# Four sums of squares split by one instruction per engine and multiplied with w_out one period later

## The chip, the cores and the metric

The kernel runs on one core of a Trainium2 chip. The metric is the device time of one execution in microseconds, the median of three runs. The engines go by the profile's names: PE is TensorE (PEld its weight loads), DVE is VectorE, ACT is ScalarE, POOL is GpSimd, and SP is the engine whose queue issues most of the transfers.

## The reference

Channel attention followed by a feed-forward layer with a squared ReLU, for 4 batches of 6080 tokens and 256 channels:

```
qn = q / (norm(q over tokens) + 1e-6);  kn likewise
a  = softmax(kn^T @ qn / tau)                 # 256 x 256 for each batch
x  = v @ a, read as 24320 rows of 256
h  = max(x @ w_in, 0)                         # 2048 columns
out = (h * h) @ w_out                         # back to 256
```

All values are float32. `w_in` and `w_out` arrive as 64-bit words that the kernel decodes.

## The kernel before, in words

The attention matrix of a batch is multiplied into `w_in`, so that each batch has its own weights W = a @ w_in, and the feed-forward layer reads v directly. Every float32 operand is split into a rounded part ("hi") and the rest ("lo"), both of the type float32r, and a product is three matmuls: hi with hi, hi with lo, lo with hi.

The tokens of a batch are cut into 12 blocks of 512 (the last two of 480). The first two blocks and the very last one are done plainly. The 45 blocks between run in 180 periods, four for each block (`groups`, with k the period and j = 0 to 3 the quarter of the 2048 hidden columns). A period forms its quarter by a Strassen-like scheme (Winograd's variant): seven products of 6 matmuls, accumulated in three PSUM banks, B2 (`h0`), H (`h1`) and C (`h2`). In the program's order these are B2 = A11 B11 and H = S1 T1; then, with C first set to a copy of B2 by ACT, C += S2 T2, B2 += A12 B21, H += S4 B22, C += S3 T3 and, last, C += A22 T4. Between them ACT and DVE take the four results a1, a0, a2, a3 out of PSUM into the tile `x` (with ReLU), and square them. The second product, with w_out, works on four sums of these squares (`first_sums`, `third_sum`, `last_sum`, on DVE) and on some of the squares themselves (the "A" parts).

The order of the work on each engine is the order in which the program issues it (`InProgramOrder`, L19 to L27: nearly every instruction has L27 as its line, so that the tiles' names tell the operations apart). The period (L1250) interleaves three periods' work:

- of period k: the seven products, the evictions, ReLU and squares, and the early A parts (`hi_A(k, early_A)`, `lo_A`);
- of period k-1: the sums, the split of the late A part, the split of the four sums in two steps (`hi_S` on ACT and `lo_S` on DVE for "S1", which is a1 and a0, and again for "S2", which is a2 and a3), `window_A(k - 1)` on PE before the last product of C, and `window_S(k - 1, "S1")` on PE at the end of the period;
- of period k-2: `window_S(k - 2, "S2")` on PE between the product H = S1 T1 and C += S2 T2.

A quarter is "plain" (`plain(k)`) when its odd pair of column groups is multiplied without the scheme: j = 0 and 1 in the first three batches, and all of the first such block. A plain quarter has 9 matmuls in `window_A` and 18 and 15 in the two halves of `window_S`; another one has 18, 12 and 12.

`after_copy(k)` (L1246) decides where ACT rounds the late A part: where it holds (the last batch, not plain), after the copy of B2 into C of the next period; elsewhere ahead of it, at the end of the period itself (L1332). In the first case DVE runs `first_sums` ahead of `lo_A`, in the other behind it.

The weights of a period come by transfers on SP's queue in two loads (`load_forms`): the early ones (A11, S1, S2) are issued two periods ahead, the late ones one period ahead; each is two transfers, hi and lo. The attention of the next batch runs beside the periods in steps that wait for named points (`side("act")`, `"mid"`, `"dve"`, `"sq"`, `"pe"`): 12 matmuls of its Gram matrix in a period, and after that the norms and the softmax. The norms (`ps_n`, L600) use B2's bank `h0`: PE forms them at the point "act", ahead of `window_A`, and DVE reads them (`nx`, L616) at the point "mid", behind the split of the sums.

After the last period the plain last block starts (L1501): its steps run beside the windows that are left over (`drained`).

Of the kernel before, what the change touches and what calls it, by code (L numbers as in the profile page):

```python
# [30 lines left out]
def kernel(  # L31
# [843 lines left out]

    def two_parts(name, tag, src):

        hi, lo = [pool.tile(list(src.shape), F32R, tag=f"{tag}_{i}", name=f"{tag}_{i}{name}", bufs=1) for i in ("hi", "lo")]

        def round_hi():  # L880
            scalar.copy(hi, src)

        def take_lo():
            vector.tensor_sub(lo, src, hi.bitcast(F32))

        return hi, lo, round_hi, take_lo

    def parts_of(b, n, r):

        hi, lo, round_hi, take_lo = two_parts(f"{b}_{n}_{r}", ("s1", "s2")[r % 2], X.pop((b, n, r)))  # L890
        round_hi()
        take_lo()
        G[b, n, r] = hi, lo
# [3 lines left out]
    def eight_products(b, n, r, part):  # L897
        t0, tn = blocks[n]
        f = 2 * r + part
        if f == 0:  # L900
            O[b, n] = ps_acc.tile([P, NC, T], F32, tag="o", name=f"ps_o{b}_{n}")
        hi, lo = (x.rearrange("p s t -> p (s t)")[:, part * tn : (part + 1) * tn] for x in G[b, n, r])
        parts = ((wo_hi, hi), (wo_lo, hi), (wo_hi, lo))
# [22 lines left out]
    def final_products(b, n, r, part):  # L926
# [6 lines left out]
        hi, lo = (x.rearrange("p s t -> p (s t)") for x in G[b, n, r])  # L933
        ends = r == NPAIR - 1
# [22 lines left out]
    OLD = 2  # L957
    ORD = 1
    AT = (0, 0, 24, 26)
    AFTER_FROM = (12, 12, 12, 0)  # L960
    FREE_FROM = (12, 12, 12, 0)
# [43 lines left out]
    def half_of(k):  # L1005
        return blocks[groups[k][1]][1] // 2
# [75 lines left out]

    def window_S(k, which):
        j = groups[k][2]
        names = {"S1": ((1, "S1n"), (2, "S3")), "S2": ((0, "S2"), (3, "A22"))}[which]
        pairs = range(1 if plain(k) else 2)
        sums = [
            (1, at, 1, weights_of(2 * j + p)[name], p, slot) for slot, (at, name) in enumerate(names) for p in pairs
        ]
        if plain(k):  # L1090
            r = 2 * j + 1
            f = int(which == "S2")
            w = [[w[:, 2 * r + f, m * P : (m + 1) * P] for w in (wo_hi, wo_lo)] for m in range(2)]
            if f == 0:
                sums += [(0, 3, 1, w[0], 1, 0), (0, 2, 1, w[0], 1, 1)]
            else:
                sums.append((0, 2, 2, w[0], 1, 0))
            for slot, side in enumerate(((1, 0), (0, 1))[f]):
                t, at = ((0, 0), (1, 3))[side]
                sums.append((t, at, 1, w[1], 1, slot))  # L1100
        to_output(k, sums, PA[k, which])

# [82 lines left out]

    SLOTS = {"S1": slice(a1, a0 + 1), "S2": slice(a2, a3 + 1)}

    def parts_tile(k, kind):
        n = 3 if kind == "A" else 2
        tag = {"A": "A", "S1": "s1", "S2": "s2"}[kind]  # L1190
        PA[k, kind] = [
            pool.tile([P, 2, n, half_of(k)], F32R, tag=f"{tag}_{i}", name=f"{tag}_{i}_{k}", bufs=1) for i in ("hi", "lo")
        ]
# [6 lines left out]
    def lo_A(k, which):  # L1200
        s, at = which
        n = 1 if plain(k) else 2
        hi, lo = (part[:, 0:n, at, :] for part in PA[k, "A"])
        vector.tensor_sub(lo, XG[k][:, 0:n, s, :], hi.bitcast(F32))

    def hi_S(k, which):
        parts_tile(k, which)
        scalar.copy(PA[k, which][0], XG[k][:, :, SLOTS[which], :])

    def lo_S(k, which):  # L1210
        hi, lo = PA[k, which]
        vector.tensor_sub(lo, XG[k][:, :, SLOTS[which], :], hi.bitcast(F32))

# [31 lines left out]

    def after_copy(k):  # L1246

        return not plain(k) and k < len(groups) - 1 and groups[k][1] >= AFTER_FROM[groups[k][0]]

    def period(k, before=nothing, w1=None, wa=None, w3=None):  # L1250

# [18 lines left out]
        if prev:  # L1270
            if ORD and after_copy(k - 1):
                first_sums(k - 1)
                lo_A(k - 1, late_A)
            else:
# [48 lines left out]
        parts_tile(k, "A")  # L1323
        hi_A(k, early_A)
# [126 lines left out]
    for g in range(len(groups)):  # L1451
        b, n, j = groups[g]
        if g == 0:
            period(
                g,
                before=lambda: parts_of(*pairs[-1]),
                w1=left_over((PAIR // 2 - 2, 0), (PAIR // 2 - 2, 1)),
                wa=left_over((PAIR // 2 - 1, 0)),
                w3=left_over((PAIR // 2 - 1, 1)),
            )  # L1460
        elif g == 1:
            period(g, w1=nothing)
        else:
            period(g)
# [5 lines left out]
    banks["turn"] = 0  # L1470
    def sums_of_last():
        first_sums(K - 1)
        lo_A(K - 1, late_A)
        third_sum(K - 1)
        last_sum(K - 1)
        hi_S(K - 1, "S1")
        lo_S(K - 1, "S1")

    def rest_of_last():
        hi_S(K - 1, "S2")  # L1480
        lo_S(K - 1, "S2")

    drained = {
        0: (
            lambda: window_S(K - 2, "S2"),
            sums_of_last,
# [3 lines left out]
        ),  # L1490
        1: (lambda: window_A(K - 1), rest_of_last),
        2: (lambda: window_S(K - 1, "S1"),),
        3: (
            lambda: window_S(K - 1, "S2"),
            lambda: copy_output(K - 1, 0),
# [51 lines left out]
```

## Time and profile before

| | us |
|---|---|
| median of 3 runs (2137.43 to 2138.04) | 2137.51 |
| span of the profiled execution | 2137.0 |
| PE busy (16990 matmuls) | 2123.9 |
| PE weight loads busy (16990) | 2066.1 |
| DVE busy (2577 instructions) | 1947.1 |
| ACT busy (2708 instructions) | 1818.6 |
| POOL busy | 403.4 |

The page names the execution by its span. Busy time is the union of an engine's instructions, so matmuls that overlap in the pipeline count once. In the timeline a line gives the start, the length, the engine, the operation and its tiles; the bracket at the end is the idle time of the engine just before, with what ended it. The granted TensorE clock is 1.000 over the span. The chain that ended last is PE for 89%, DVE for 6%, ACT and the transfers for 2% each.

### The profile page before, as it was taken

What the parts mean: (1) busy time and instruction counts of PE and PEld (TensorE: products, weight loads), DVE (VectorE), ACT (ScalarE), POOL (GpSimd) and SP (SyncE); (2) the same over time, 40 slices, a digit from 0 to 9 for tenths busy, and PEclk for the clock granted to TensorE, in tenths of its full rate; (3) what the DMA queues carried; (4) which work ended last, traced back from release to release, by engine and by line L of the source; (5) the groups of instructions that cost most, each with busy time, mean ns of one, the idle gap of its engine ahead of it and who ended that gap; (6) DMA issues with size and microseconds to landing.
All of it is one profiled execution on the core that took longest, in us unless ns stands there. A gap on an engine that the chain in (4) does not pass through costs nothing.

```text
span 2137.0 us, 43905 instructions
## 1 busy us (share of the span) xinstructions
PE 2123.9 (99%) x16990; PEld 2066.1 (97%) x16990; DVE 1947.1 (91%) x2577; ACT 1818.6 (85%) x2708; POOL 403.4 (19%) x506
## 2 busy tenths in 40 slices
PE   9999999999999999999999999999999999999999
PEld 8789999999999999999999999999999999999998
DVE  6898999998999999988999999999899999999993
ACT  5887888888888888878888888878888999999995
POOL 0000121211222121221222121121212122122121
PEclk9999999999999999999999999999999999999999
DMA  9777888889998888788999788887999788788783
GB/s 345 234 232 264 240 255 252 235 239 283 303 297 262 251 251 262 234 241 247 292 303 288 248 255 257 249 234 229 325 322 314 233 241 252 220 247 248 233 256 86
DMA packets 258865, 548.24 MB, mean 257 GB/s; under 512 B 26848, under 2 KB 120672, under 8 KB 258656
## 3 DMA queue, kind: packets, MB, share of 16 engines
q1 hardware_dynamic: 193696, 449.32, 62.3%
q0 software_dynamic: 64960, 96.11, 20.9%
q8 instruction: 134, 2.20, 0.4%
q14 instruction: 75, 0.61, 0.1%
HBM read 431.75 MB, written 64.23 MB: 232 GB/s over the span
## 4 chain that ended last, share of the span: by engine, by line
PE 89%; DVE 6%; ACT 2%; DMA 2%; issue 1%; SPq 0%; DVEq 0%; ACTq 0%
PE ps_o L27 41%; PE ps_c L27 16%; PE ps_h L27 14%; PE ps_b L27 11%; PE gram L27 4%; DVE x L27 2%; PE ps_w L27 2%; PE ps_o_m L27 1%; ACT x L27 1%; DMA wf<-wf_kept 1%; DVE s_lo L27 1%; DVE acc L27 1%; DMA qk<-in_k 1%; DVE A_lo L27 0%; DMA qk<-in_q 0%
## 5 line engine op out<-in xcount | busy, mean ns | idle before, releaser
L27 DVE TENSOR_TENSOR s_lo<-x,s_hi 128x1024 fp32r<-128x1024 f32 (+1 forms) x384 | 464.0, 1208 | 44.4 <-ACT s_hi L27 44.1
L27 PE MATMUL ps_c<-v_hi,wf 128*128 128x256 f32 (+1 forms) x2160 | 466.9, 280 | 4.4 <-DVE x L27 2.2
L27 POOL DMA_DIRECT2D o<-o x225 | 245.4, 1253 | 1102.7 <-ACT o L27 689.7
L27 ACT CAST s_hi<-x 128x1024 fp32r<-128x1024 f32 (+1 forms) x384 | 399.7, 1041 | 37.6 <-DVE x L27 27.9
L27 DVE TENSOR_TENSOR x<-x 128x1024 f32<-128x1024 f32 (+3 forms) x540 | 389.6, 722 | 10.3
L27 PEld LDWEIGHTS ps_c<-v_hi,wf 128*128 128x128 f32 x2160 | 367.4, 188 | 7.8 <-ACT ps_c L27 3.3
L27 ACT ACTIVATE x<-x 128x512 f32<-128x512 f32 (+2 forms) x540 | 350.0, 648 | 21.7 <-DVE x L27 9.2
L27 PE MATMUL ps_b<-v_hi,wf 128*128 128x256 f32 (+1 forms) x1440 | 309.7, 279 | 1.8 <-DVE nx L27 1.1
L27 PE MATMUL ps_h<-v_hi,wf 128*128 128x256 f32 (+1 forms) x1440 | 309.1, 278 | 0.0
L27 PE MATMUL ps_c<-v_lo,wf 128*128 128x256 f32 (+1 forms) x1080 | 300.9, 279 | 0.0
L27 DVE TENSOR_TENSOR A_lo<-x,A_hi 128x1024 fp32r<-128x1024 f32 (+3 forms) x360 | 276.9, 792 | 18.8 <-ACT A_hi L27 15.3
L27 ACT CAST A_hi<-x 128x1024 fp32r<-128x1024 f32 (+3 forms) x360 | 254.4, 707 | 38.4 <-DVE x L27 25.5
L27 PEld LDWEIGHTS ps_b<-v_hi,wf 128*128 128x128 f32 x1440 | 245.2, 188 | 2.3 <-DVE nx L27 1.3
L27 PEld LDWEIGHTS ps_h<-v_hi,wf 128*128 128x128 f32 x1440 | 244.9, 188 | 0.0
L27 ACT COPY x<-ps_c 128x512 f32<-128x512 f32 (+1 forms) x180 | 105.1, 584 | 158.3 <-PE ps_c L27 158.0
L27 PEld LDWEIGHTS ps_c<-v_lo,wf 128*128 128x128 f32 x1080 | 203.2, 188 | 0.1
L27 PE MATMUL ps_b<-v_lo,wf 128*128 128x256 f32 (+1 forms) x720 | 200.6, 279 | 0.0
L27 PE MATMUL ps_h<-v_lo,wf 128*128 128x256 f32 (+1 forms) x720 | 200.4, 278 | 0.0
L27 DVE TENSOR_TENSOR x<-x,ps_h 128x512 f32<-128x512 f32 (+1 forms) x180 | 122.4, 680 | 76.9 <-PE ps_h L27 76.6
L27 PE MATMUL ps_o<-s_hi,wo_hi 128*128 128x256 f32 (+3 forms) x954 | 190.1, 295 | 0.5 <-ACT s_hi L27 0.5
L27 PE MATMUL ps_o<-s_hi,wo_lo 128*128 128x256 f32 (+3 forms) x954 | 190.2, 295 | 0.0
L27 PE MATMUL ps_o<-s_lo,wo_hi 128*128 128x256 f32 (+3 forms) x954 | 190.0, 295 | 0.1
(166 smaller groups left out, 5166.9 us busy)
## 6 DMA issues: line engine op xcount, KB each, us to landing
wf<-wf_kept SPq DMA_DIRECT2D x360, 512.0 KB, 5.3
wf<-wf_kept SPq DMA_DIRECT2D x360, 384.0 KB, 4.9
o<-o POOLq DMA_DIRECT2D x114, 256.0 KB, 5.9
qk<-in_k SPq DMA_DIRECT2D x87, 256.0 KB, 4.3
qk<-in_q SPq DMA_DIRECT2D x87, 256.0 KB, 4.8
v<-in_vT POOLq DMA_DIRECT2D x76, 256.0 KB, 5.1
out_T<-o POOLq DMA_DIRECT2D x152, 128.0 KB, 4.7
o<-o POOLq DMA_DIRECT2D x76, 128.0 KB, 6.2
```

What stands on the lines that cost most here:

```text
L27: return lambda *args, **kwargs: self.tc.keep_in_program_order(issue(*args, **kwargs))
```

## The change

The split of the four sums becomes one instruction on ACT (`scalar.copy` of 128x2048) and one on DVE (`tensor_sub` of 128x2048), from and into one pair of tiles `s_parts` in place of the four tiles of "S1" and "S2". Both come later in the period: `hi_S(k - 1)` behind the eviction of a0 and the copy of the second half of an output, `lo_S(k - 1)` behind `relu_squares`. For that `last_sum` is always done with `third_sum`, ahead of the addition of H to a1. `window_S` is one window, placed where the "S2" half stood: in period k it multiplies the sums of k-2. The window at the period's end is gone. `after_copy` is gone: the late A part is rounded behind the copy of B2 into C, and `first_sums` runs ahead of `lo_A`, in all periods. The plain blocks at the beginning and the end use halves of `s_parts`; the last block has a third pair of buffers, in the place of A's tiles. The drained windows at the end move with it.

```
-    def window_S(k, which):
+    def window_S(k):
...
         sums = [
-            (1, at, 1, weights_of(2 * j + p)[name], p, slot) for slot, (at, name) in enumerate(names) for p in pairs
+            (1, at, 1, weights_of(2 * j + p)[name], p, slot)
+            for at, name, slot in ((1, "S1n", a1), (2, "S3", a0), (0, "S2", a2), (3, "A22", a3))
+            for p in pairs
         ]
...
-    def hi_S(k, which):
-        parts_tile(k, which)
-        scalar.copy(PA[k, which][0], XG[k][:, :, SLOTS[which], :])
-
-    def lo_S(k, which):
-        hi, lo = PA[k, which]
-        vector.tensor_sub(lo, XG[k][:, :, SLOTS[which], :], hi.bitcast(F32))
+    def hi_S(k):
+        half = half_of(k)
+        PA[k, "S"] = [part[:, : 8 * half].rearrange("p (r s t) -> p r s t", r=2, s=4) for part in s_parts]
+        scalar.copy(PA[k, "S"][0], XG[k])
+
+    def lo_S(k):
+        hi, lo = PA[k, "S"]
+        vector.tensor_sub(lo, XG[k], hi.bitcast(F32))
...
         scalar.copy(C[:, :, :half], B2[:, :, :half])
-        if prev and after_copy(k - 1):
+        if prev:
             hi_A(k - 1, late_A)
...
         if prev:
-            if ORD and after_copy(k - 1):
-                first_sums(k - 1)
-                lo_A(k - 1, late_A)
-            else:
-                lo_A(k - 1, late_A)
-                first_sums(k - 1)
+            first_sums(k - 1)
+            lo_A(k - 1, late_A)
         side("dve")
         late_step(last=True)
         if prev:
             third_sum(k - 1)
-            if plain(k - 1):
-                last_sum(k - 1)
+            last_sum(k - 1)
         v_step(k, "dve")
-        (w1 or (lambda: window_S(k - 2, "S2")))()
+        (w1 or (lambda: window_S(k - 2)))()
...
         product(k, B2, A12, B21)
-        if prev:
-            hi_S(k - 1, "S1")
         scalar.activation(x[:, :, a0, :], B2[:, :, :half], AF.Relu)
         if w1 is None:
             copy_output(k - 2, 1)
+        if prev:
+            hi_S(k - 1)
         product(k, H, S4, B22)
...
-        if prev and not plain(k - 1):
-            last_sum(k - 1)
         product(k, C, S3, T3)
...
         side("sq")
-        if prev:
-            lo_S(k - 1, "S1")
-            hi_S(k - 1, "S2")
         square(k, a0)
         relu_squares(k)
         if prev:
-            lo_S(k - 1, "S2")
+            lo_S(k - 1)
...
         square(k, a2)
-        if not after_copy(k):
-            hi_A(k, late_A)
-        (w3 or (lambda: window_S(k - 1, "S1")))()
```

## Rows read from the trace of the kernel before

**Rows 1.** The page's head and its part 1: busy time, share of the span and instructions of each engine.
```profile
span 2137.0 us, 43905 instructions
...
PE 2123.9 (99%) x16990; PEld 2066.1 (97%) x16990; DVE 1947.1 (91%) x2577; ACT 1818.6 (85%) x2708; POOL 403.4 (19%) x506
```

**Rows 2.** Busy time in a stretch, here the periods: the stretch, its length, busy us and instructions of each engine, granted clock, transfer share, GB/s.
```profile
160.00:2076.00 1916.00, 1909.32 (x15982) 1887.76 (x15981) 1790.92 (x2381) 1663.09 (x2511) 383.86 (x476) 1.00 0.85 260
```

**Rows 3.** Waits of PE's weight loads in the periods (160 to 2076 us): who waited, for whom, us in total, times, the longest.
```profile
PEld ps_c L27 <- ACT ps_c L27: 3.3, 6, 1.1
PEld ps_c L27 <- DVE x L27: 3.2, 5, 1.1
PEld ps_b L27 <- DVE nx L27: 1.3, 1, 1.3
PEld ps_b L27 <- DMA wf<-wf_kept: 0.9, 1, 0.9
```

**Rows 4.** Timeline, DVE and PE, about 416 to 418.5 us (the norms of the second batch, between two periods). The first two lines are DVE, the others PE.
```profile
416.43 1.22 DVE L27 TENSOR_TENSOR s_lo<-x,s_hi 128x1024 fp32r<-128x1024 f32 x1
417.56 0.15 DVE L27 TENSOR_SCALAR nx<-ps_n 128x4 f32<-128x4 f32 x1
...
416.36 0.39 PE L27 MATMUL ps_o<-s_hi,wS_hi 128*128 128x256 f32 x2
...
418.45 0.28 PE L27 MATMUL ps_b<-v_hi,wf 128*128 128x256 f32 x1
```

**Rows 5.** The same for the third batch's norms, 919 to 927 us.
```profile
919.71 0.69 DVE L27 TENSOR_TENSOR x<-x,ps_h 128x512 f32<-128x512 f32 x1 [1.09 <-PE ps_h L27]
920.32 0.68 DVE L27 TENSOR_TENSOR x<-x 128x512 f32<-128x512 f32 x1
...
926.64 0.15 DVE L27 TENSOR_SCALAR nx<-ps_n 128x4 f32<-128x4 f32 x1
...
924.17 0.28 PE L27 MATMUL ps_o<-s_hi,wS_hi 128*128 128x256 f32 x1
...
926.85 0.38 PE L27 MATMUL ps_b<-v_hi,wf 128*128 128x256 f32 x1 [1.11 <-DVE nx L27]
```

**Rows 6.** The same for the fourth batch's norms, 1429 to 1431.5 us.
```profile
1430.48 0.15 DVE L27 TENSOR_SCALAR nx<-ps_n 128x4 f32<-128x4 f32 x1
...
1429.28 0.40 PE L27 MATMUL ps_o<-s_hi,wS_hi 128*128 128x256 f32 x2
...
1431.40 0.28 PE L27 MATMUL ps_b<-v_hi,wf 128*128 128x256 f32 x1
```

**Rows 7.** Timeline, PE, 1134 to 1137 us (end of a period and begin of the next).
```profile
1134.50 0.27 PE L27 MATMUL ps_o<-s_hi,wS_hi 128*128 128x240 f32 x1
...
1135.84 0.28 PE L27 MATMUL ps_b<-v_hi,wf 128*128 128x256 f32 x1
...
1136.96 0.50 PE L27 MATMUL ps_b<-v_hi,wf 128*128 128x256 f32 x2 [0.73 <-DMA wf<-wf_kept]
```

**Rows 8.** Timeline, PE, 628 to 630.5 us; then the transfers issued from 622.6 to 622.8 us and from 624.4 to 624.6 us (the early weights, hi and lo, of the period that begins at 630.27: issuer, count, size, us from issue to landing).
```profile
628.15 0.40 PE L27 MATMUL ps_o<-s_hi,wS_hi 128*128 128x256 f32 x2
...
630.27 0.28 PE L27 MATMUL ps_b<-v_hi,wf 128*128 128x256 f32 x1
...
wf<-wf_kept SPq DMA_DIRECT2D x1, 384.0 KB, 5.7
...
wf<-wf_kept SPq DMA_DIRECT2D x1, 384.0 KB, 5.5
```

**Rows 9.** Groups of instructions by form over the span: DVE's and ACT's splits, x the count, then busy us, mean ns of one, idle before.
```profile
L27 DVE TENSOR_TENSOR s_lo<-x,s_hi 128x1024 fp32r<-128x1024 f32 x320 | 390.3, 1220 | 15.1 <-ACT s_hi L27 15.0
...
L27 ACT CAST s_hi<-x 128x1024 fp32r<-128x1024 f32 x320 | 335.9, 1050 | 20.9 <-DVE x L27 20.8
...
L27 DVE TENSOR_TENSOR A_lo<-x,A_hi 128x512 fp32r<-128x512 f32 x152 | 104.3, 686 | 11.9 <-ACT A_hi L27 11.7
...
L27 ACT CAST A_hi<-x 128x512 fp32r<-128x512 f32 x152 | 94.6, 622 | 18.5 <-DVE x L27 11.3 <-PE ps_c L27 5.5
```

**Rows 10.** Timeline, ACT, 725 to 737 us: a period with j = 3 in the stretch in which the Gram matrix runs beside, up to the copy of B2 into C of the next period.
```profile
726.31 1.05 ACT L27 CAST s_hi<-x 128x1024 fp32r<-128x1024 f32 x1
...
727.97 1.30 ACT L27 ACTIVATE x<-x 128x512 f32<-128x512 f32 x2
729.17 1.05 ACT L27 ACTIVATE qk<-qk 128x1024 f32<-128x1024 f32 x1
730.12 1.03 ACT L27 CAST s_hi<-x 128x1024 fp32r<-128x1024 f32 x1
...
734.77 0.62 ACT L27 CAST A_hi<-x 128x512 fp32r<-128x512 f32 x1
735.29 0.58 ACT L27 COPY ps_c<-ps_b 128x512 f32<-128x512 f32 x1
```

**Rows 11.** The same stretch on DVE (third sum, addition of H to a1, last sum), and the matmul on PE that waits for the copy.
```profile
726.33 0.68 DVE L27 TENSOR_TENSOR x<-x 128x512 f32<-128x512 f32 x1
727.24 0.69 DVE L27 TENSOR_TENSOR x<-x,ps_h 128x512 f32<-128x512 f32 x1 [0.23 <-PE ps_h L27]
727.85 0.68 DVE L27 TENSOR_TENSOR x<-x 128x512 f32<-128x512 f32 x1
...
736.09 0.28 PE L27 MATMUL ps_c<-v_hi,wf 128*128 128x256 f32 x1
```

More of the change, by code (lines that the diff above doesn't have):

```diff
@@ L874, in squares @@
         scalar.activation(x, x, AF.Square)
[L876 to L886, printed above, removed]
-    def parts_of(b, n, r):
-        hi, lo, round_hi, take_lo = two_parts(f"{b}_{n}_{r}", ("s1", "s2")[r % 2], X.pop((b, n, r)))
-        round_hi()
-        take_lo()
+    s_parts = [pool.tile([P, 4 * T], F32R, tag=f"s_{i}", name=f"s_{i}", bufs=1) for i in ("hi", "lo")]
+    def parts_of(b, n, r):
+        src = X.pop((b, n, r)).rearrange("p s t -> p (s t)")
+        tn = blocks[n][1]
+        at = r % 3 if (b, n) == order[-1] else r % 2
+        if at == 2 and "A" not in G:
+            G["A"] = [pool.tile([P, 2 * tn], F32R, tag=f"A_{i}", name=f"A_{i}_last", bufs=1) for i in ("hi", "lo")]
+        hi, lo = G["A"] if at == 2 else (part[:, 2 * tn * at : 2 * tn * (at + 1)] for part in s_parts)
+        scalar.copy(hi, src)
+        vector.tensor_sub(lo, src, hi.bitcast(F32))
         G[b, n, r] = hi, lo
@@ L901, in eight_products @@
             O[b, n] = ps_acc.tile([P, NC, T], F32, tag="o", name=f"ps_o{b}_{n}")
-        hi, lo = (x.rearrange("p s t -> p (s t)")[:, part * tn : (part + 1) * tn] for x in G[b, n, r])
+        hi, lo = (x[:, part * tn : (part + 1) * tn] for x in G[b, n, r])
         parts = ((wo_hi, hi), (wo_lo, hi), (wo_hi, lo))
@@ L932, in final_products @@
                 final[m] = ps_acc.tile([P, T], F32, tag="o", name=f"ps_o{b}_{n}_m{m}")
-        hi, lo = (x.rearrange("p s t -> p (s t)") for x in G[b, n, r])
+        hi, lo = G[b, n, r]
         ends = r == NPAIR - 1
@@ L957 @@
     OLD = 2
-    ORD = 1
     AT = (0, 0, 24, 26)
-    AFTER_FROM = (12, 12, 12, 0)
     FREE_FROM = (12, 12, 12, 0)
@@ L1091, in window_S @@
             r = 2 * j + 1
[L1092 to L1095, printed above, removed]
-            else:
[L1097 to L1101, printed above, removed]
+            w = [[[w[:, 2 * r + f, m * P : (m + 1) * P] for w in (wo_hi, wo_lo)] for m in range(2)] for f in range(2)]
+            sums += [(0, 3, 1, w[0][0], 1, a1), (0, 2, 1, w[0][0], 1, a0), (0, 2, 2, w[1][0], 1, a2)]
+            sums += [(1, 3, 1, w[0][1], 1, a1), (0, 0, 1, w[0][1], 1, a0)]
+            sums += [(0, 0, 1, w[1][1], 1, a2), (1, 3, 1, w[1][1], 1, a3)]
+        to_output(k, sums, PA[k, "S"])
     def copy_output(k, t):
@@ L1184, in last_sum, with parts_of_A @@
         sum_of(k, a3, a3, a2, vector.tensor_sub)
[L1186 to L1192, printed above, removed]
+    def parts_of_A(k):
+        PA[k, "A"] = [
+            pool.tile([P, 2, 3, half_of(k)], F32R, tag=f"A_{i}", name=f"A_{i}_{k}", bufs=1) for i in ("hi", "lo")
         ]
@@ L1244, in v_step, with period @@
         next(vprep[0], None)
-    def after_copy(k):
-        return not plain(k) and k < len(groups) - 1 and groups[k][1] >= AFTER_FROM[groups[k][0]]
-    def period(k, before=nothing, w1=None, wa=None, w3=None):
+    def period(k, before=nothing, w1=None, wa=None):
         now["k"] = k
@@ L1270, in period @@
         if prev:
-            if ORD and after_copy(k - 1):
-                first_sums(k - 1)
-                lo_A(k - 1, late_A)
-            else:
-                lo_A(k - 1, late_A)
-                first_sums(k - 1)
+            first_sums(k - 1)
+            lo_A(k - 1, late_A)
         side("dve")
@@ L1322, in period @@
         (wa or (lambda: window_A(k - 1)))()
-        parts_tile(k, "A")
+        parts_of_A(k)
         hi_A(k, early_A)
@@ L1458 @@
                 wa=left_over((PAIR // 2 - 1, 0)),
-                w3=left_over((PAIR // 2 - 1, 1)),
             )
         elif g == 1:
-            period(g, w1=nothing)
+            period(g, w1=left_over((PAIR // 2 - 1, 1)))
         else:
@@ L1471, in sums_of_last @@
     def sums_of_last():
+        hi_A(K - 1, late_A)
         first_sums(K - 1)
@@ L1475, in sums_of_last @@
         last_sum(K - 1)
[L1476 to L1481, printed above, removed]
+        hi_S(K - 1)
+        lo_S(K - 1)
     drained = {
         0: (
-            lambda: window_S(K - 2, "S2"),
+            lambda: window_S(K - 2),
             sums_of_last,
@@ L1490 @@
         ),
-        1: (lambda: window_A(K - 1), rest_of_last),
-        2: (lambda: window_S(K - 1, "S1"),),
+        1: (lambda: window_A(K - 1),),
         3: (
-            lambda: window_S(K - 1, "S2"),
+            lambda: window_S(K - 1),
             lambda: copy_output(K - 1, 0),
```

1 line of the change is left out of this document (removed).

## The prediction

> **What bounds the kernel now.** I read the page's busy times first, then the busy time of the periods alone, then what PE waited for in them, and only then single periods in the timeline. The page shows PE busy for 2123.9 of 2137.0 us, DVE for 91% and ACT for 85% [rows 1]. From 160 to 2076 us PE is busy for 1909.3 of 1916.0 us, so that 6.7 us are idle there, while DVE has 125 us and ACT 253 us to spare [rows 2]. PE's matmuls start one behind the other at 0.116 us for 256 columns: 18 of them from 416.36 to 418.45 us [rows 4]. So PE sets the end. The change leaves the count and the form of its matmuls as they are; it can move the time only by PE's waits. Those in the periods are few: its weight loads waited 3.3 us in 6 places for ACT's copy of B2 into C, 3.2 us in 5 places for DVE, 1.3 us once for DVE's reading of the norms and 0.9 us once for a transfer of weights [rows 3]. A gain can come from the first two only. The reader is to look for the places where a wait that is now hidden loses its cover.
>
> **What moves on PE.** From C += A22 T4 of a period to B2 = A11 B11 of the next PE now has the "S1" window to do: 18 matmuls (2.09 us) behind a plain quarter [rows 4], 12 behind another (1.40 us at 0.1165). After the change B2 stands directly behind the last product of C, and these matmuls come 12 matmuls later. All anchors from C += S2 T2 on keep their distance, since A and both halves of S still lie between one H += S4 B22 and the next. So the deadlines of B2 = A11 B11 alone are 1.4 to 2.1 us earlier, and whatever is ready less than that ahead of it now is late. B2's bank is free by then in an ordinary period (its eviction lies before `window_A`). Two kinds of producer are not.
>
> **The norms.** In three periods, one for each of the batches 2 to 4, the bank holds `ps_n` until DVE has read it, at a point behind the split of the sums.
> - 417 us: DVE reads at 417.56, PE is through with A22 at 416.36 and has the S1 window until 418.45 as cover [rows 4]. Without it B2 starts when the reading has ended. DVE's order up to there is the same work, 0.07 us shorter (below): 417.56 - 0.07 + 0.15 and 0.06 for the release, which is what lies between the end of the reading at 926.79 and the matmul at 926.85 [rows 5], is 417.70. PE waits for 1.34 us.
> - 1430 us: the same, 1430.48 - 0.07 + 0.15 + 0.06 = 1430.62 against 1429.28 [rows 6]: 1.34 us.
> - 926 us: B2 waits already, until 926.85 [rows 5]. The S1 window of 1.40 us that is done before this now comes after it. Against that DVE comes there earlier: `last_sum` (0.61 us from the start of the one before) now stands between the additions of H and C to the results; moved ahead it falls into 1.09 us in which DVE waits for PE [rows 5]. I take 0.50 of it, as the addition of C can't start before its product is done, and 0.07 from the split: 1.40 - 0.57 = 0.83 us.
> Together 3.5 us; at least 2.5 (if DVE gains 0.4 us in each), at most 4.1 (no gain at all).
>
> **The weights.** The early weights are wanted by B2 = A11 B11, and their transfers are issued by SP behind other work, not by PE's new order.
> - 1136 us: the third matmul of B2 waits for the lo half until 1136.96; the S1 window lay from 1134.50 to 1135.84 [rows 7]. The landing stays where it is, so the 1.34 us come on top.
> - 628 us: B2 starts at 630.27 and would start at 628.15; the hi half, issued at about 622.7, lands 5.7 us later, at 628.4, and the lo half, issued at about 624.45, 5.5 us later, at 629.95 [rows 8]. The third matmul, 0.23 us behind the first, then starts at 630.0 in place of 628.38: 1.6 us.
> Together 3.0 us; none if SP's queue comes to these loads 2 us earlier (it waits there for DVE steps that gain some 0.1 to 0.3 us, so hardly), 4 if the load at 1136 is late by one more us.
>
> **The split by one instruction.** No instruction of 128x2048 is in the trace. On DVE 128x512 takes 686 ns and 128x1024 takes 1220, on ACT 622 and 1050 [rows 9]; continued on the same line, 2048 takes 2288 and 1906 ns. What counts is the distance of starts: 1.13 us on DVE for 1024 [rows 4], 0.95 on ACT [rows 10], 0.09 and 0.10 less than the duration. So two now cost 2.27 and 1.90 us, one then 2.20 and 1.80: 0.07 and 0.10 us saved in a period, 12 and 18 us over 180. The bounds are no saving (two starts) and the whole fixed part, 1220 - 2 x 534 = 152 ns and 1050 - 2 x 428 = 194 ns. All of it lies beside PE. [...]
>
> **The order on ACT and DVE.** The late A part's rounding goes behind the copy of B2 into C: 0.52 us earlier for the copy [rows 10]. But the first half of the split now runs while ACT would stand idle: at 726.31, ahead of the relu that waits for DVE's addition at 727.97 [rows 10]. The one instruction has to wait for `last_sum`. DVE's row has third sum, addition, last sum at 726.33, 727.24 and 727.85 [rows 11]; moved ahead, the last sum ends at about 727.5. The split then runs from 727.6 to 729.4, and the relu follows 1.4 us later than before. What was behind it loses the second split (0.95 us) and the rounding (0.52 us and the wait for the square that feeds it, some 0.1). Net: the copy starts 0 to 0.2 us earlier than at 735.29. It is done at 735.87 and wanted at 736.09 [rows 10, 11], so 0.2 us of slack hold in this kind of period, of which a batch has about six beside its Gram matrix, 18 in three batches. Where DVE is later, as in the places of the six waits, I expect the copy between 0.5 us earlier and 0.3 us later, 0.7 us won over the six; from DVE's waits 0.15 us in each of five, 0.7 us; and 0.6 us from DVE's other short delays of PE. Together 2.0 us won; the bounds are all of the 6.5 us [rows 3], and 2 us lost.
>
> `lo_A` and `first_sums` change places at no cost: the same DVE work, and what waits for it (third sum, `window_A`) is behind both. The S window's operands are ready a whole half period before it starts, so the later splits cost PE nothing; the cover is PE's own B2 and H. The copies of the outputs and the third buffer pair of the last block stand on ACT and DVE where PE has work. POOL's and SP's queues are passed by nothing new.
>
> **The sum.** 3.5 + 3.0 - 2.0 = 4.5 us on the profiled execution's 2137.0 us, 2141.5; the median of the runs lies 0.5 us above that execution, so 2142.0 us, 0.21% more. PE's later work is as tight as its earlier one, so that a wait of B2 isn't won back by the next period.
>
> **The rivals.**
> - *The give-back cancels it.* DVE's and ACT's savings remove all their 6.5 us of waits [rows 3], and B2's new waits are as worked out: 2137.5 + 6.5 - 6.5 = 2137.5 us; halfway, 2139.5. For it: the copy is no longer behind the rounding. Against it: the split's wait for `last_sum`.
> - *Faster.* B2's producers come in time, and the DVE and ACT waits go: 2137.5 - 6.5 = 2131.0 us. This decides at B2 = A11 B11: the reading of the norms would have to come 1.3 us earlier than rows 4 and 6 have it, and the weights 1.3 to 1.6 us. DVE is busy without a gap ahead of the reading, so I give it little. [...]
> - *The rounding stalls ACT.* If the one split ends more than 0.2 us later than I have it, the copy of B2 is late in all 18 periods with j = 3 of the Gram stretches, and in some beside: 0.5 us late costs 18 x (0.5 - 0.2) = 5.4 us, so 2147.4 us. For it: only 0.2 us of slack [rows 10, 11]. Against it: the rounding moved away.
>
> **How the numbers follow.** About 0.2% (4.3 us) can be told from no change here. My forecast (2139.5 to 2144.5, its own range) gets 0.50, split 0.27 above 2141.8 and 0.23 below; the cancelling 0.25, all within; faster 0.10, of which 0.09 below 2133.2; the stalled rounding 0.15, above. That makes faster 0.09, same 0.48, slower 0.43. The range that leaves out the outer two tenths goes from 2134.5 to 2147.5.
>
> **What would show it.** Right: in the changed kernel PE's weight loads wait for `nx` three times, 1.3, 2.6 and 1.3 us, and for the early weights twice, 1.6 and 2.2 us, all at `ps_b`; the waits of `ps_c` for ACT and DVE are no longer than 5 us together; s_hi and s_lo of 2048 take about 1.91 and 2.29 us. Wrong: no wait of `ps_b` for `nx` at the second and the fourth batch, or many short waits of `ps_c` for ACT in the Gram stretches, or a busy PE whose matmuls no longer start at 0.116 us.

## The result, and the profile after

The changed kernel took 2154.99 us, the median of 4 runs (2153.67 to 2157.6), against 2137.47 us for the kernel before (2137.35 to 2138.04) beside it: a ratio of 1.0080, with a 95% interval of 1.0066 to 1.0094. I had forecast 2142.0 us and a range up to 2147.5. The direction was right, the size was not: 17.5 us in place of 4.5. Run again later, beside other kernels, it took 2153.44 us (ratio 1.0072, 1.0059 to 1.0085).

The page's head and its part 1 after the change, to be held against [rows 1]:

```profile
span 2155.5 us, 43631 instructions
...
PE 2129.4 (99%) x16990; PEld 2070.4 (96%) x16990; DVE 1967.9 (91%) x2397; ACT 1794.4 (83%) x2528; POOL 402.7 (19%) x506
```

PE has the same 16990 matmuls. ACT is 24 us less busy and DVE 21 us more, although each has 180 instructions fewer. Where PE's weight loads wait in the periods (160 to 2094 us; who waited, for whom, us in total, times, the longest), against [rows 3]:

```profile
PEld ps_c L27 <- ACT ps_c L27: 10.5, 18, 1.4
PEld ps_b L27 <- DVE nx L27: 6.3, 3, 2.5
PEld ps_c L27 <- DVE x L27: 3.4, 6, 1.4
PEld ps_b L27 <- DMA wf<-wf_kept: 2.9, 2, 1.7
```

The waits for the copy of B2 into C are up by 7.2 us, those for the norms by 5.0, those for the early weights by 2.0: 14.2 of the 18.5 us between the two profiled executions. The clock, in the last section of this text, accounts for an estimated 1.6 us more. Ahead of the periods this execution lost 2.1 us: its first B2 starts at 160.50 us, in the kernel before at 158.44, and its granted clock was 0.50 from about 9.2 to 12.6 us. The repetition, 2.8 us shorter, starts its first B2 at 158.79 and has a mean granted clock of 0.999, against 0.998 here; its waits for the early weights come to 1.9 us in place of 2.9. The splits by form (busy us, mean ns of one, then the idle time of the engine before them and what ended it), against [rows 9]:

```profile
L27 DVE TENSOR_TENSOR s_lo<-x,s_hi 128x2048 fp32r<-128x2048 f32 x152 | 347.6, 2287 | 2.1
...
L27 ACT CAST s_hi<-x 128x2048 fp32r<-128x2048 f32 x152 | 290.6, 1912 | 91.0 <-DVE x L27 89.5
```

The durations are those that I had worked out (2288 and 1906 ns). What is new is the last column: ACT stands idle for 89.5 us ahead of its one rounding, until a sum on DVE is done. Ahead of the two roundings before it was 20.8 us [rows 9].

One period with j = 3 beside the Gram matrix in the timeline of the changed kernel, to be held against [rows 10, 11]: ACT, then DVE, then PE.

```profile
735.63 0.60 ACT L27 ACTIVATE x<-ps_b 128x512 f32<-128x512 f32 x1
737.54 1.91 ACT L27 CAST s_hi<-x 128x2048 fp32r<-128x2048 f32 x1 [1.30 <-DVE x L27]
739.35 1.29 ACT L27 ACTIVATE x<-x 128x512 f32<-128x512 f32 x2
...
742.95 1.05 ACT L27 CAST A_hi<-x 128x1024 fp32r<-128x1024 f32 x1
...
745.06 0.58 ACT L27 COPY ps_c<-ps_b 128x512 f32<-128x512 f32 x1
...
736.09 1.41 DVE L27 TENSOR_TENSOR x<-x 128x512 f32<-128x512 f32 x2
737.42 0.68 DVE L27 TENSOR_TENSOR x<-x,ps_h 128x512 f32<-128x512 f32 x1
738.02 0.68 DVE L27 TENSOR_TENSOR x<-x,ps_c 128x512 f32<-128x512 f32 x1
738.74 0.69 DVE L27 SCALAR_TENSOR_TENSOR x<-x 128x512 f32<-128x512 f32 x1
...
744.02 1.23 DVE L27 TENSOR_TENSOR A_lo<-x,A_hi 128x1024 fp32r<-128x1024 f32 x1 [1.12 <-ACT A_hi L27]
...
745.01 0.39 PE L27 MATMUL ps_o<-s_lo,wo_hi 128*128 128x256 f32 x2
745.68 0.39 PE L27 MATMUL ps_c<-v_hi,wf 128*128 128x256 f32 x1 [0.28 <-ACT ps_c L27]
```

Read from the top. ACT is free at 736.23 and waits 1.30 us for the last sum (the second of the two at 736.09). The rounding takes 1.91 us; behind it come the relu of a1 (739.35), the squares, the rounding of the early A part (742.95) and the copy of B2 into C (745.06). The copy ends at 745.64; PE was through with the S window's matmuls two starts after 745.01, at 745.24, and begins C += S2 T2 at 745.68 only. DVE in turn stood idle for 1.12 us until ACT had rounded the A part. The same wait comes back after every four periods, that is, after every block:

```profile
697.93 1.23 DVE L27 TENSOR_TENSOR A_lo<-x,A_hi 128x1024 fp32r<-128x1024 f32 x1 [1.12 <-ACT A_hi L27]
...
790.13 1.23 DVE L27 TENSOR_TENSOR A_lo<-x,A_hi 128x1024 fp32r<-128x1024 f32 x1 [1.12 <-ACT A_hi L27]
...
836.24 1.23 DVE L27 TENSOR_TENSOR A_lo<-x,A_hi 128x1024 fp32r<-128x1024 f32 x1 [1.12 <-ACT A_hi L27]
```

Between 697.93 and 744.02, and again in the two blocks after it, DVE has no idle time above 0.11 us. At the end of such a stretch ACT goes without a gap from its rounding at 737.54, which waited for the last sum, to the rounding of the A part that ends at 744.00. This closes a circle between the two engines: DVE's work up to the last sum, ACT's from there to the A part, then DVE again. One turn takes 46.1 us. PE's own work in four periods is shorter: in the kernel before H = S1 T1 starts at 688.44, 733.99 and 779.53, 45.55 us apart, in the changed kernel at 741.75, 787.88 and 833.99, 46.1 us apart. In this stretch the circle sets the pace, and PE loses some 0.56 us in each block.

### The profile page after: what moved, and what is told of

Read it like the earlier page. It is cut to its first block, busy times and chain, and to the rows that moved or that the text cites. A ratio compares the mean times of both kernels' runs of the same rounds, so it can differ in the third digit from the quotient of the medians.

```text
span 2155.5 us, 43631 instructions
## 1 busy us (share of the span) xinstructions
PE 2129.4 (99%) x16990; PEld 2070.4 (96%) x16990; DVE 1967.9 (91%) x2397; ACT 1794.4 (83%) x2528; POOL 402.7 (19%) x506
## 4 chain that ended last, share of the span: by engine, by line
PE 85%; DVE 6%; ACT 5%; DMA 2%; issue 1%; SPq 0%; DVEq 0%; ACTq 0%
PE ps_o L27 38%; PE ps_c L27 15%; PE ps_h L27 13%; PE ps_b L27 10%; PE gram L27 6%; DVE x L27 2%; PE ps_w L27 2%; ACT x L27 2%; DVE s_lo L27 1%; PE ps_o_m L27 1%; ACT A_hi L27 1%; ACT qk L27 1%; ACT qk_hi L27 1%; DVE A_lo L27 1%; DMA wf<-wf_kept 1%
## 5 line engine op out<-in xcount | busy, mean ns | idle before, releaser
L27 DVE TENSOR_TENSOR s_lo<-x,s_hi 128x2048 fp32r<-128x2048 f32 (+3 forms) x202 | 434.5, 2151 | 33.4 <-ACT s_hi L27 29.1
L27 ACT CAST s_hi<-x 128x2048 fp32r<-128x2048 f32 (+3 forms) x202 | 363.7, 1801 | 99.5 <-DVE x L27 97.7
L27 ACT ACTIVATE x<-x 128x512 f32<-128x512 f32 (+2 forms) x540 | 341.3, 643 | 8.6
L27 DVE TENSOR_TENSOR A_lo<-x,A_hi 128x1024 fp32r<-128x1024 f32 (+3 forms) x360 | 284.9, 791 | 24.1 <-ACT A_hi L27 24.0
L27 DVE SCALAR_TENSOR_TENSOR x<-x 128x1024 f32<-128x1024 f32 (+3 forms) x180 | 177.4, 986 | 6.2
L27 PE MATMUL ps_o<-s_hi,wo_hi 128*128 128x256 f32 (+3 forms) x954 | 178.8, 295 | 0.5 <-ACT s_hi L27 0.5
L27 PE MATMUL ps_o<-s_hi,wo_lo 128*128 128x256 f32 (+3 forms) x954 | 178.7, 295 | 0.0
L27 PE MATMUL ps_o<-s_lo,wo_hi 128*128 128x256 f32 (+3 forms) x954 | 178.7, 295 | 0.1
```

The costliest lines, as they stand in the source:

```text
L27: return lambda *args, **kwargs: self.tc.keep_in_program_order(issue(*args, **kwargs))
```

## The experiments

All were timed beside the kernel before, whose median in the four groups of runs was 2138.22, 2138.32, 2137.78 and 2138.05 us. The theories at the outset: A, the one split that waits for the last sum makes the copy late, and the merged window takes B2's cover; B, the new order of copy, rounding and first sums is at fault.

### The order, the splits and the windows, each alone

**The order alone**, in the kernel before:

```
-        return not plain(k) and k < len(groups) - 1 and groups[k][1] >= AFTER_FROM[groups[k][0]]
+        return k < len(groups) - 1
```

> The kernel before with the new order alone (late A part rounded behind the copy, first sums ahead of its rest, in all periods; two splits, two windows). Theory A, the one split that waits for the last sum makes the copy of B2 late, and the merged window takes B2's cover: this kernel has neither, so 2136 to 2139 us, and the waits of ps_c for ACT stay at about 3 us. Theory B, the order itself makes ACT or DVE late: about 2145 us, with 8 to 10 us of waits of ps_c for ACT.

Measured: 2138.20 us, ratio 1.0001 (0.9992 to 1.0010). PE's waits from 160 to 2076 us:

```profile
PEld ps_c L27 <- DVE x L27: 4.1, 6, 1.5
PEld gram L27 <- DVE qk_lo L27: 2.4, 3, 1.3
PEld ps_b L27 <- DVE nx L27: 1.7, 1, 1.7
PEld ps_c L27 <- ACT ps_c L27: 1.0, 3, 0.5
```

The copy gains as intended (3.3 us of waits become 1.0), and DVE's products lose as much: the two waits for DVE and the one for the norms are 0.9, 1.8 and 0.4 us longer. Theory B falls.

**Two splits** in the changed kernel, at their old places, with the window together:

```
             third_sum(k - 1)
-            last_sum(k - 1)
+            if plain(k - 1):
+                last_sum(k - 1)
...
         product(k, B2, A12, B21)
+        if prev:
+            hi_S(k - 1, "S1")
...
-        if prev:
-            hi_S(k - 1)
         product(k, H, S4, B22)
...
+        if prev and not plain(k - 1):
+            last_sum(k - 1)
         product(k, C, S3, T3)
...
         side("sq")
+        if prev:
+            lo_S(k - 1, "S1")
+            hi_S(k - 1, "S2")
...
-            lo_S(k - 1)
+            lo_S(k - 1, "S2")
```

> The changed kernel with the split done again in two steps, the first ahead of the relu of a0, the last sum behind the addition of H (windows stay together a period later, order new). Theory A: the waits of ps_c for ACT fall from 10.5 to about 3 us and with them the time by 8 to 10 us, to 2145 to 2147 us; the waits of ps_b for nx (6 us) and for the early weights (3 us) stay. Theory B: it stays at 2153 to 2157 us.

Measured: 2145.44 us, ratio 1.0032 (1.0019 to 1.0044):

```profile
PEld ps_b L27 <- DVE nx L27: 6.0, 3, 3.1
...
PEld ps_b L27 <- DMA wf<-wf_kept: 1.1, 2, 0.7
PEld ps_n L27 <- ACT x L27: 0.8, 3, 0.3
PEld ps_c L27 <- ACT ps_c L27: 0.5, 1, 0.5
```

As theory A has it: the copy is in time again, 8.0 to 9.6 us are won against the two readings of the changed kernel, and the waits of `ps_b` stay. Against the order alone, the merged window costs 7.2 us.

**Two windows** in the changed kernel, the first half at the period's end again, with one split:

```
-        (w1 or (lambda: window_S(k - 2)))()
+        (w1 or (lambda: window_S(k - 2, "S2")))()
...
         square(k, a2)
+        if prev:
+            window_S(k - 1, "S1")
```

> The changed kernel with the window in two halves again, the first at the period's end, ahead of the next B2 (one split, new order). Theory A: the cover of B2 is back, the waits of ps_b for nx fall from 6.3 to about 1.5 us and those for the early weights from 2.9 to about 1, the waits of ps_c for ACT stay at about 10: 2155 less 6 to 7 = 2148 to 2149 us. My forecast's reading, by which B2's waits are the whole loss: 2138 to 2141 us.

Measured: 2214.93 us, ratio 1.0358 (1.0344 to 1.0373). Neither reading had that:

```profile
PEld ps_o L27 <- DVE s_lo L27: 67.0, 102, 1.5
...
PEld ps_c L27 <- ACT ps_c L27: 1.2, 3, 0.5
PEld ps_b L27 <- DVE nx L27: 1.1, 1, 1.1
```

The waits of `ps_b` do fall to 1.1 us, but a window at the period's end needs the subtraction, and DVE's one subtraction ends too late for it in 102 places. With the one subtraction at this place in DVE's order, the earlier window can't be kept. The short waits for the copy say nothing here, as the longer wait ahead of them gives ACT time.

**The old order** in the changed kernel (rounding at the period's end, `lo_A` ahead of `first_sums`):

```
-        if prev:
+        if prev and after_copy(k - 1):
             hi_A(k - 1, late_A)
...
-            first_sums(k - 1)
-            lo_A(k - 1, late_A)
+            if after_copy(k - 1):
+                first_sums(k - 1)
+                lo_A(k - 1, late_A)
+            else:
+                lo_A(k - 1, late_A)
+                first_sums(k - 1)
...
         square(k, a2)
+        if not after_copy(k):
+            hi_A(k, late_A)
```

> The changed kernel with the old order (late A part rounded at the period's end and ahead of the copy, its rest ahead of the first sums, except in the last batch). Theory A: the copy comes later still, by up to the 0.5 us of the rounding in the 18 periods in which it is late: 2155 to 2164 us. Theory B: 2145 to 2148 us.

Measured: 2157.48 us, ratio 1.0086 (1.0073 to 1.0100).

```profile
PEld ps_c L27 <- ACT ps_c L27: 16.7, 24, 1.4
```

With the rounding ahead of it the copy is late in 24 places, and its waits come to 6.2 us more. The time is only 2.5 to 4.0 us above the two readings of the changed kernel, as other waits are shorter. The new order is no cause of the loss here either; if anything it makes it smaller.

### Which of the two engines

Theory A is now split in two. A1: the place and the wait of the rounding on ACT are the cost. A2: DVE's own order is the cost, that is, the last sum moved ahead and the one subtraction.

**ACT's rounding in two, at the old places**, DVE's subtraction in one:

```
         product(k, B2, A12, B21)
+        if prev:
+            hi_S(k - 1, "S1")
...
         side("sq")
+        if prev:
+            hi_S(k - 1, "S2")
```

> The changed kernel with ACT's rounding of the four sums in two instructions at the old places (a1 and a0 ahead of the relu of a0, a2 and a3 at the point sq); DVE's subtraction stays one instruction, the last sum stays ahead of the addition of H. Theory A1, ACT's place and wait are the cost (it stands still for the last sum and then holds the relu and the squares for 1.9 us): 2144 to 2147 us, as with two splits on both engines, and waits of ps_c for ACT of about 1 us. Theory A2, DVE's order is the cost (one subtraction of 2.3 us, last sum ahead of the addition): 2152 to 2157 us.

Measured: 2197.74 us, ratio 1.0286 (1.0271 to 1.0300); both theories missed. DVE's waits from 160 to 2076 us:

```profile
DVE s_lo L27 <- ACT s_hi L27: 87.4, 74, 1.9
```

One subtraction needs both halves, and at that place the second half comes only behind the relu and the square of a1.

**ACT's one rounding moved behind the relu and the square of a1:**

```
-        if prev:
-            hi_S(k - 1)
         product(k, H, S4, B22)
...
         side("sq")
+        if prev:
+            hi_S(k - 1)
```

> The changed kernel with ACT's one rounding moved behind the relu and the square of a1, to the point sq, so that ACT doesn't stand still for the last sum ahead of them. Theory A1 in its narrow form (the 1.3 us in which ACT waits for the last sum are lost): ACT is ahead again, the waits of ps_c for ACT fall from 10.5 to under 4 us, 2145 to 2150 us. In its wide form (1.9 us in one piece on ACT makes DVE's early A part wait wherever it stands): the wait moves to DVE's subtraction, and the time stays at 2152 to 2158 us or above.

Measured: 2259.84 us, ratio 1.0568 (1.0554 to 1.0582): the wide form, and far above the changed kernel.

```profile
DVE s_lo L27 <- ACT s_hi L27: 138.0, 68, 2.8
```

**DVE's subtraction in two**, the first ahead of `relu_squares`, ACT's rounding in one:

```
         side("sq")
+        if prev:
+            lo_S(k - 1, "S1")
...
-            lo_S(k - 1)
+            lo_S(k - 1, "S2")
```

> The changed kernel with DVE's subtraction in two (a1 and a0 at the point sq, ahead of relu_squares; a2 and a3 behind it), ACT's rounding in one. Theory A1: no gain, as ACT is late as before, and the first half now waits for the rounding some 0.7 us: 2155 to 2175 us. Theory A2 with the one subtraction as the cause: 2146 to 2150 us.

Measured: 2231.22 us, ratio 1.0437 (1.0423 to 1.0450), the sign of theory A1, but 76 us above the changed kernel where it allowed 20 at most:

```profile
DVE s_lo L27 <- ACT s_hi L27: 123.0, 161, 1.3
```

These three show the same thing: DVE has little room to wait. Waits of 87, 123 and 138 us made the kernel 43, 76 and 105 us slower than the changed one (from 2154.99), half to three quarters of the wait each time.

**ACT's rounding in two, the second half where the one instruction stood**, DVE as in the changed kernel:

```
         product(k, B2, A12, B21)
+        if prev:
+            hi_S(k - 1, "S1")
...
         if prev:
-            hi_S(k - 1)
+            hi_S(k - 1, "S2")
         product(k, H, S4, B22)
```

> The changed kernel with ACT's rounding of the sums in two: a1 and a0 ahead of the relu of a0, where ACT stood idle; a2 and a3 where the one instruction stood, ahead of the relu of a1. DVE as in the changed kernel (last sum ahead of the addition of H, one subtraction). Theory A1 (the 1.9 us on ACT that can't begin before the last sum pass to the early A part, and DVE waits for that): the relu of a1 comes some 0.85 us earlier, DVE's waits for A_hi fall from 23 us to under 8, waits of ps_c for ACT from 10.5 to under 4: 2145 to 2149 us. Theory A2 (DVE's own order, last sum ahead and one subtraction): 2152 to 2157 us.

Measured: 2141.30 us, ratio 1.0020 (1.0012 to 1.0029), 12.1 to 13.7 us less than the changed kernel and less than theory A1 expected. PE's waits for the copy, DVE's for the A part and ACT's for the sum (160 to 2076 us):

```profile
PEld ps_c L27 <- ACT ps_c L27: 0.6, 1, 0.6
...
DVE A_lo L27 <- ACT A_hi L27: 11.1, 25, 1.9
...
ACT s_hi L27 <- DVE x L27: 22.4, 49, 1.7
```

In the changed kernel the last two are 23.4 and 95.1 us. The same kind of period as above, ACT and then PE:

```profile
729.00 1.05 ACT L27 CAST s_hi<-x 128x1024 fp32r<-128x1024 f32 x1
...
730.72 1.05 ACT L27 CAST s_hi<-x 128x1024 fp32r<-128x1024 f32 x1 [0.17 <-DVE x L27]
731.67 1.29 ACT L27 ACTIVATE x<-x 128x512 f32<-128x512 f32 x2
...
737.38 0.58 ACT L27 COPY ps_c<-ps_b 128x512 f32<-128x512 f32 x1
...
738.77 0.28 PE L27 MATMUL ps_c<-v_hi,wf 128*128 128x256 f32 x1
```

The half that needs the first sums alone fills ACT's idle time (729.00), 0.17 us of waiting are left, and the copy starts 1.39 us ahead of its matmul, in place of 0.18 us (745.24 less 745.06). The four periods take 45.55 us again (H = S1 T1 at 689.73, 735.27 and 780.82), so that the circle no longer sets the pace. Theory A1 holds: the cost was on ACT, and it was the half that had been made to wait for a sum which it doesn't read. Of the gain, this execution shows 9.9 us in the waits for the copy, 1.0 us in those for the norms (5.3 in place of 6.3 us), and the 1.6 us of clock of the last section, as behind its 2.0 us of idle time at the third batch's norms the clock doesn't fall (its mean is 1.000, in the changed kernel 0.998).

**The last sum ahead of the addition of H** in the kernel with two splits:

```
             third_sum(k - 1)
-            if plain(k - 1):
-                last_sum(k - 1)
+            last_sum(k - 1)
...
-        if prev and not plain(k - 1):
-            last_sum(k - 1)
         product(k, C, S3, T3)
```

> The kernel with two splits and the window together (2145.4 us), with the last sum ahead of the addition of H as in the changed kernel. Theory A1: the addition is 0.7 us later, which the old slack and ACT's idle time take up in part: 2145 to 2148 us. Theory A2 with the last sum as the cause: 2151 to 2156 us.

Measured: 2146.28 us, ratio 1.0045 (1.0032 to 1.0058), as A1 has it. Its profiled execution ran at a granted clock of 0.947, so its rows aren't read.

### The norms

**The norms read ahead of the subtraction**, in the kernel with two splits, in the kernel before with the new order (in both behind the first subtraction), and in the changed kernel (ahead of the one):

```
-        yield from step(b, 1, "act")
+        yield from step(b, 1, "sq")
         ps_n = ps_h.tile([P, T], F32, tag="h0", name=f"ps_n{b}") if b else bank(f"ps_n{b}")
...
-        yield from step(b, 2, "mid")
+        yield from step(b, 2, "norms")
...
         relu_squares(k)
+        norms()
         if prev:
             lo_S(k - 1)
```

> The kernel with two splits and the window together (2145.4 us), and DVE reads the norms right behind the first subtraction, some 2.4 us earlier; PE forms them at the same place. If the waits of ps_b for nx (6.0 us) are what the merged window costs: 2139 to 2141 us, and nx gone from the list of waits. If the next period is late anyway (what ps_b waited for hides another producer that is late by as much): 2144 to 2146 us.

Measured: 2136.99 us, ratio 0.9995 (0.9986 to 1.0004): 8.4 us less, more than the 6.0 us of waits.

> The kernel before with the new order alone (2138.2 us), and the norms read 2.4 us earlier. One wait of 1.7 us at ps_b should go: 2136.3 to 2137 us. If another producer is late behind it: 2138 us.

Measured: 2136.65 us, ratio 0.9990 (0.9981 to 0.9999).

> The changed kernel with the norms read 2.3 us earlier, ahead of the subtraction. If nx is all that the merged window cost and adds to the late copies: 2146 to 2149 us, nx gone from the waits of ps_b. If the late copies and nx overlap (a period that is late anyway): 2151 to 2155 us.

Measured: 2145.12 us, ratio 1.0037 (1.0024 to 1.0050), 8.3 to 9.9 us less than the changed kernel, with the copy as late as it was:

```profile
PEld ps_c L27 <- ACT ps_c L27: 11.0, 19, 1.4
...
PEld ps_b L27 <- DMA wf<-wf_kept: 0.9, 2, 0.5
```

So the reading of the norms, with the clock behind it, is the price of the merged window: without it the window together (2136.99) and in halves (2136.65) are the same. The two losses add up nearly: taken away singly they give 12.1 and 8.3 us against the repetition, together (next section) 18.2. The 2.2 us between are about the 1.6 us of clock, which each remedy takes away by itself: the profiled execution of each has a mean granted clock of 1.000, those of the changed kernel and its repetition 0.998 and 0.999.

### Both remedies

**The changed kernel with ACT's rounding in two and the norms read early:**

> The changed kernel with both remedies: ACT's rounding in two (the first half ahead of the relu of a0) and the norms read ahead of the subtraction. If these two account for the whole loss: 2141.3 less 5 to 7, 2134 to 2137 us, no slower than the kernel before, waits of ps_b for nx and of ps_c for ACT together under 2 us. If something else in the changed order costs too: 2138 to 2142 us.

Measured: 2135.24 us, ratio 0.9987 (0.9978 to 0.9996). In the list of PE's waits `nx` is gone, and the copy has 0.6 us in one place. No other loss from the change shows in the time, though 2.1 us of waits for the early weights are left in this execution; a remedy for them was not tried. It has the lowest median, 2.8 us below the kernel before. But the early norms aren't part of the change: with them and the new order alone the kernel before was already 1.7 us lower (2136.65 against 2138.32), and the intervals of the two ratios overlap. That the one split and the merged window gain anything is thus not shown.

**The same with DVE's subtraction as two instructions**, one behind the other:

```
-        vector.tensor_sub(lo, XG[k], hi.bitcast(F32))
+        for at in SLOTS.values():
+            hi, lo = (part[:, :, at, :] for part in PA[k, "S"])
+            vector.tensor_sub(lo, XG[k][:, :, at, :], hi.bitcast(F32))
```

> The same with DVE's subtraction as two instructions, one right behind the other, at the place of the one. If DVE's 0.07 us in a period are worth something where DVE is all but full (the Gram stretches): 1 to 4 us above the kernel with one subtraction. If they are hidden: the same within 1 us.

Measured: 2137.25 us, ratio 0.9997 (0.9988 to 1.0005). The page's part 1 of the kernel with one subtraction, and then of this one:

```profile
PE 2120.3 (99%) x16990; PEld 2064.6 (97%) x16990; DVE 1964.9 (92%) x2397; ACT 1788.9 (84%) x2708; POOL 403.0 (19%) x506
```

```profile
PE 2120.6 (99%) x16990; PEld 2065.3 (97%) x16990; DVE 1975.8 (93%) x2577; ACT 1788.7 (84%) x2708; POOL 402.6 (19%) x506
```

DVE is busy 10.9 us longer, and the median is 2.0 us higher; 10 of its 11 runs lie above the median of the other, though the intervals of the two overlap. That DVE's 10.9 us make the 2 us isn't shown: in its profiled execution PE's weight loads also waited 2.3 us once for ACT (`ps_c` for `x`), in place of 1.1 us once with one subtraction, and the mean granted clock was 0.999 in place of 1.000.

## Why the prediction was wrong

**The step that failed** is the one on the order on ACT: "Net: the copy starts 0 to 0.2 us earlier than at 735.29". What comes between the relu of a1 and the copy I had right. I had 1.57 us less of it (0.95, 0.52 and 0.1), and the traces have 735.29 - 727.97 = 7.32 us before [rows 10] and 745.06 - 739.35 = 5.71 after, 1.61 less. The start of the relu was wrong: I had it 1.4 us later. Counted back from the matmul that wants the copy, it stood 736.09 - 727.97 = 8.12 us ahead before [rows 10, 11] and 745.24 - 739.35 = 5.89 after, 2.23 us later. The missing 0.8 us lie in the last sum. I let it end at 727.5, 8.6 us ahead of that matmul; it ended at 737.50, 7.7 ahead. Of this, 0.6 us lie in the start of the third sum (9.15 us ahead of the matmul in place of 9.76) and 0.24 in the two sums themselves, which take 1.41 us from start to end where I had counted 1.17. I had taken DVE's times of the old period and put the new instruction among them. But DVE's times depend on ACT: a later rounding of the early A part makes DVE wait (1.12 us), and as it has no idle time in the four periods that follow, the last sum at the end of them is late too. So the copy was late in 18 places in place of 6, and its waits rose by 7.2 us, where I had booked 2.0 us won for this term. With the rounding in halves 12 to 14 us come back, more than those waits; its trace accounts for most of the rest by the norms and the clock.

My third rival named this, place and mechanism. I gave it 0.15, and priced it at 18 places of 0.3 us. That the list has 18 places too is chance: ten of them lie behind a period with j = 3 in a Gram stretch and weren't late before, with 5.1 us together, 0.5 us a place; the others lie elsewhere, some of them late already before. Against it stood that the rounding moves away. The order alone shows that this helps (3.3 to 1.0 us), but less than the wait for the last sum costs.

**The norms** were named with the right three places and were too small: 3.5 us for 5.0. At 417 us I had 1.34 us; the place after the change, DVE and then PE:

```profile
418.05 0.69 DVE L27 TENSOR_TENSOR x<-x,ps_h 128x512 f32<-128x512 f32 x1 [1.25 <-PE ps_h L27]
...
422.75 0.15 DVE L27 TENSOR_SCALAR nx<-ps_n 128x4 f32<-128x4 f32 x1
...
421.01 0.28 PE L27 MATMUL ps_c<-v_hi,wf 128*128 128x256 f32 x1
422.96 0.39 PE L27 MATMUL ps_b<-v_hi,wf 128*128 128x256 f32 x1 [1.67 <-DVE nx L27]
```

B2 could start one matmul (0.12 us) after 421.01 and starts 1.83 us later than that. From the addition of H to the reading DVE takes 4.70 us. Before, the reading came 4.63 us after the addition, which began at 412.93 in that trace. I had counted on 0.07 less, not more: `relu_squares` now follows directly on the addition whose result it reads (last section). Most of the rest is on PE's side: forming the norms waited 0.8 us in three places for ACT's relu of a0, which stood behind the first rounding (it still does with two splits, `ps_n` in that list). After the change the relu comes first, and this wait of some 0.27 us is gone: PE is ready for B2 3.08 us behind the start of that addition, before it was 3.43. A wait that goes on PE moves a deadline forward. For the second place the 2.6 us that I had named came out (2.5), but by luck: my own terms, the 1.3 us of before and 0.83 more, make 2.1. What I hadn't counted at all is the clock behind it, below.

**The weights**: 3.0 us forecast, 2.0 more than before in this trace. Without any edit to them the list has 2.9 us in the changed kernel, 1.9 in its repetition, 1.1 with two splits, 0.9 with the norms read early and 2.1 with both remedies: two places each time, but a landing that isn't the same from one execution to the next. I had taken one execution's landing for a fixed time.

**The split's durations** were right, and so was the saving of one start: 12 us of DVE time forecast, 10.9 us measured (1975.8 less 1964.9, the last experiment). The whole fixed part of my line, 152 ns in each of 180 periods, would have been an estimated 27 us. That the saving shows on PE at all isn't certain. **The sum** of 4.5 us thus had its first two terms nearly right together (6.5 forecast, 7.0 measured in waits), by luck in part, as one was 1.5 us too small and the other 1.0 too large; the third had the wrong sign, and the clock wasn't in it.

## What to carry to other kernels

An instruction that is merged from two has the later of their two inputs and the earlier of their two deadlines; before merging, see what each half filled. Where two engines feed each other, follow a delay once around the circle, to where the same place comes again (here four periods later), and hold the length of one turn against the own work of the engine that sets the pace, before pricing it at one place. When a block of work is moved away from in front of a wait, list every producer that had it as cover, and price each with the deadline after the change.

## What was not expected of the hardware

**The clock.** At the norms of the third batch PE's wait was the longest. Stretches of the changed kernel (stretch, length, busy us and count of PE, PEld, DVE, ACT and POOL, granted clock, transfer share, GB/s), then PE:

```profile
934.00:937.60 3.60, 1.42 (x13) 1.22 (x11) 3.50 (x6) 1.85 (x3) 0.00 (x0) 1.00 0.64 212
937.60:941.00 3.40, 3.25 (x15) 3.25 (x16) 2.84 (x11) 1.17 (x3) 0.00 (x0) 0.50 0.52 206
941.00:945.00 4.00, 4.00 (x36) 4.00 (x36) 0.67 (x2) 1.73 (x3) 0.00 (x0) 1.00 0.00 0
```

```profile
937.75 0.58 PE L27 MATMUL ps_b<-v_hi,wf 128*128 128x256 f32 x1 [2.33 <-DVE nx L27]
...
941.09 0.28 PE L27 MATMUL ps_o<-s_hi,wo_hi 128*128 128x256 f32 x1
```

After 2.33 us in which PE stood idle the granted clock was 0.50 for 3.4 us, and then 1.00 again. The 15 matmul starts from 937.75 to 941.09 took 3.34 us, where 15 at 0.1165 take 1.75: by this estimate the wait cost 1.6 us beyond itself. The repetition has a fall behind its 2.3 us at this place (0.61 in the mean from 937.0 to 940.5 us), the kernel with two splits behind 2.87 us (0.50 from 928.8 to 932.0 us). Behind the 1.67 us of idle time at 422.96 the clock stayed at 1.00 (422.9 to 427.0 us), and also behind the 1.11 us at this place before [rows 5] (926.85 to 930.0 us). With ACT's rounding in halves PE stood idle for 2.0 us there, and no matmul of `ps_b` with `v_lo` from 919 to 950 us took over 0.281 us, where the first two of the changed kernel behind its wait took 0.42 and 0.41. But the length of the idle time doesn't tell it alone: with the old order PE stood idle for 2.3 us at this place, as in the repetition, and those matmuls took at most 0.281 us too; and in the changed kernel's first section the clock was at 0.50 from about 9.2 to 12.6 us, behind 1.63 us in which PE waited for a transfer. The fall at the norms is a part of what the early norms gave back beyond their waits: with them the mean clock is 1.000, in the kernel with two splits as in the changed kernel, without them 0.999 and 0.998.

**Instructions that depend on the one before.** In the period above DVE's addition to a1 and the one to a3, which don't touch each other, start 0.60 us apart (737.42, 738.02). The `relu_squares` behind them, of the same size, reads the second's result and starts 0.72 us after it (738.74). I had priced by the distance of independent starts alone. The change puts two such pairs directly behind each other: the addition to a3 and `relu_squares` in each period, and the third and the last sum in each period that isn't plain (in the plain ones they stood so before). At 0.12 us each that is an estimated 0.24 us in a period that isn't plain, against 0.07 saved by the one subtraction. Two kernels of the experiments can be held beside this, with the same 2577 instructions on DVE and the norms read early in both: with two splits at the old places, without the pairs, DVE was busy for 1954.7 us, with the pairs and the two subtractions one behind the other for 1975.8 us, 21.1 us more (ACT's rounding stands elsewhere too). The one subtraction takes 10.9 of them away. The new order alone, without these pairs, has 7.9 us more than the kernel before (1955.0 for 1947.1). Together, 18.1 us, this is most of the 21 us by which DVE's busy time rose with 180 instructions fewer.
